# Router logits by 8 products a tile instead of 12, and six tiles' logits planned with a margin

## The chip, the cores and the metric

One core of a Trainium2 chip runs the kernel. The metric is the device time of one execution in microseconds, as the median of several runs; the profile is of one execution of its own.

## The reference

Three layers follow each other. The first is an attention between 512 tokens and 32 state rows, both ways, in 8 batches of 8 heads. Its output, 4352 tokens of 512 values, goes through a dense layer with squared ReLU. The last layer is a mixture of 8 experts in which each token takes one, chosen by logits of normalised vectors:

```
h = x @ w_in; g = relu(h)**2; x = g @ w_out              # 512 -> 2048 -> 512

xn = x / (norm(x) + 1e-6); en = emb / (norm(emb) + 1e-6)
logits = xn @ en.T / tau                                 # 8 experts
e = argmax(logits); w = softmax(logits)[e]
out = w * (relu(x @ w1[e]) @ w2[e])                      # 512 -> 1024 -> 512
```

What the change touches is `xn @ en.T`: for each tile of 128 tokens, 512 values times 8 expert embeddings.

## The kernel before, in words

The 4352 tokens are 34 tiles of 128. Float32 operands are split into a high and a low float16 half, and a product of two such operands is three float16 products (high x high, high x low, low x high) that add up in PSUM.

Up to about 700 us several strands run interleaved. The attention of batch b (`attention`, `state_side`, `state_w`) makes the inputs of two units of 256 tokens: `aT`, transposed by DMA, and `sw` (state times `w_in`, products of line 692). `up1` multiplies them (lines 1387 to 1389, 12 products for two columns of hidden tiles), `hidden` squares the result on ACT and VectorE, and `down1` multiplies by `w_out` (lines 1471 to 1473; the first four tiles in float32, line 1450). Beside this, ACT and VectorE split the experts' weights and write them back to memory (`w_d<-he`). From about 700 us on the second mixture runs: 35 steps of gathered tokens (lines 1781 to 1806).

`route_tile` (line 1204) takes a finished tile of `down1`: ACT squares it and sums (line 1211), VectorE makes a scale, ACT and VectorE split it into two halves (lines 322 and 317), SP issues a DMA transpose into `xr` (line 1225), a single buffer, and TensorE makes the logits: for each of 4 pieces of 128 values, the high half of `xr` times `en_h`, the same times `en_l`, and the low half times `en_h`, all into 8 columns of one PSUM tile (lines 1234 to 1236). VectorE copies them (line 1239). After four tiles `route_group` (line 1243) picks the experts and GpSimd writes the token records.

The order on each engine isn't written out. Each strand is a generator that yields what it needs next: an engine and a duration, an event, or a buffer. `Plan.run` keeps a clock for each engine and takes the strand that can start first by its estimates, then the one with the lower priority number; the instructions are issued to the engines in that order. For TensorE work of strands with a priority from 1.3 to below 5 it adds `MARGIN` (1.75 us) to the time at which the data are believed ready:

```
dep = r[2] if len(r) > 2 else th[2]
if r[0] == "pe" and 1.3 <= th[1] < 5:
    dep += self.MARGIN
key = (max(dep, self.free[r[0]]), th[1])
```

`end` in `down1` starts `route_tile` with priority 2 for tiles 4 to 31, and with 0 for the first four and the last two.

Of the kernel before, what the change touches and what calls it, by code (L numbers as in the profile page):

```python
# [11 lines left out]
F16 = mybir.dt.float16  # L12
# [4 lines left out]
ALU = mybir.AluOpType  # L17
X = mybir.AxisListType.X
# [5 lines left out]
NE, FE = 8, 1024  # L24
# [200 lines left out]
def act(n):  # L225
    return "act", 0.1 + 0.83e-3 * n
# [10 lines left out]
def tiny(k):  # L237
    return "dve", TINY * k


def pe(k, n):
    return "pe", k * max(0.004, n * 0.4163e-3)
# [3 lines left out]
def moe_kernel(  # L246
# [19 lines left out]
    plan = Plan()  # L266
# [4 lines left out]
    const = ctx.enter_context(tc.tile_pool(name="const", bufs=1))  # L271
# [18 lines left out]
    mm = nc.tensor.matmul  # L290
    V = nc.vector
# [3 lines left out]
    def pow2(s, inv, v, K):  # L295

        m = small.tile([128, 4], F32, name="p2m")[:, :v.shape[1]]
        V.tensor_scalar(out=m.bitcast(I32), in0=v.bitcast(I32), scalar1=0x7F000000, scalar2=1,
                        op0=ALU.bitwise_and, op1=ALU.logical_shift_right)
        V.tensor_scalar(out=s.bitcast(I32), in0=m.bitcast(I32), scalar1=-1.0, scalar2=float(K << 23),  # L300
                        op0=ALU.mult, op1=ALU.add)
        V.tensor_scalar(out=inv.bitcast(I32), in0=m.bitcast(I32), scalar1=float((254 - K) << 23), scalar2=None,
                        op0=ALU.add)
# [15 lines left out]
    def split(hi, lo, src, scale, n):  # L319

        yield act(n)
        nc.scalar.activation(out=hi, in_=src, func=AF.Copy, scale=scale)
        yield dve(n)
        split_lo(lo, src, scale, hi)
# [48 lines left out]
    ise = const.tile([128, 2 * NE], F32, name="ise")  # L373
    u1 = const.tile([128, NT], F32, name="u1")
    itau = const.tile([128, 1], F32, name="itau")
    en_h = const.tile([128, 4, NE], F16, name="en_h")
    en_l = const.tile([128, 4, NE], F16, name="en_l")
    cum = const.tile([128, NT + 1, NE], F16, name="cum")
    nc.gpsimd.memset(cum[:, 0, :], 0.0)

# [20 lines left out]
    def ev(*key):  # L401
        return evs.setdefault(key, Ev(plan))
# [801 lines left out]
    def route_tile(i, ps, k_h, rc, st):  # L1204

        j = i % 4
        rc = rc.bitcast(F16)
        if i < 2 * F32U:
            yield ev("wo scale")
        yield act(600)  # L1210
        nc.scalar.activation(out=rc[:, 0:512].bitcast(BF16), in_=ps, func=AF.Square, accum_out=st["f2"][:, j:j + 1],
                             scale=unit if i < 2 * F32U else 1.0)
        yield tiny(4)
        f2 = st["f2"][:, j:j + 1]
        V.tensor_scalar(out=f2, in0=f2, scalar1=FLOOR, scalar2=None, op0=ALU.max)
        s2 = small.tile([128, 1], F32, name="s2")
        pow2(s2, st["is2"][:, j:j + 1], f2, 204)
        if i < 2 * F32U:
            V.tensor_tensor(out=s2, in0=s2, in1=unit, op=ALU.mult)
        yield from split(rc[:, 0:512], rc[:, 512:1024], ps, s2, 600)  # L1220
        d_slots.release(k_h)
        yield xr_slots
        yield "sp", 0.06
        xr = mg.tile([128, 8, 128], F16, name="xr", bufs=XR)
        nc.sync.dma_start_transpose(xr, rc[:, 0:1024])
        plan.cur[2] = plan.dma(1 << 18) + 1.0
        yield ev("en")
        at = plan.now()
        yield t_slots
        plan.cur[2] = max(at, plan.now())  # L1230
        pl = ps_t.tile([128, 512], F32, name="t")
        yield pe(12, NE)
        for k in range(4):
            mm(pl[:, 0:NE], lhsT=xr[:, k, :], rhs=en_h[:, k, :], start=k == 0, stop=False)
            mm(pl[:, 0:NE], lhsT=xr[:, k, :], rhs=en_l[:, k, :], start=False, stop=False)
            mm(pl[:, 0:NE], lhsT=xr[:, 4 + k, :], rhs=en_h[:, k, :], start=False, stop=k == 3)
        xr_slots.release()
        yield tiny(1)
        V.tensor_copy(st["lg"][:, j, :], pl[:, 0:NE])
        t_slots.release()  # L1240
        ev("lg", i).set()

# [162 lines left out]
    def down1():  # L1405
# [25 lines left out]
        def end(i, ps, k_h, rec, st, m):  # L1431
            g = i // 4
            if i % 4 == 0:
                plan.add(group_unscale(g), 1)
            plan.add(route_tile(i, ps, k_h, rec, st), 2 if 2 * F32U <= i < NXT else 0)
            if i % 4 == m - 1:
                plan.add(route_group(4 * g, m, st["recs"], st["k_r"], st), 2 if g < B else 0)
# [491 lines left out]
```

## Time and profile before

| | us |
|---|---|
| median of 3 runs | 1087.84 |
| lowest and highest run | 1084.52, 1088.25 |
| the profiled execution, its own time | 1086.77 |
| span of its trace | 1085.0 |
| TensorE busy in the span | 1042.6 |
| VectorE, ACT, GpSimd busy | 667.6, 593.7, 121.6 |

The busy share of TensorE is of modelled ends, and products overlap: what a product costs is the distance from its start to the next one's. The three lines of the logits have 136 products each, 34 tiles times 4.

### The profile page before, as it was taken

The page shows a single profiled execution, that of the slowest core. Times are in us where ns is not written, and L with a number is a line of the kernel's source. Part 1 is how long each engine was busy: PE and PEld are TensorE (multiplying, and loading weights), DVE is VectorE, ACT ScalarE, POOL GpSimd, SP SyncE. Part 2 cuts the span into 40 slices and gives each one's busy share as a digit, 9 for nine tenths or more (in the row PEclk, how much of TensorE's full clock was granted, in tenths as well). Part 3 has the DMA queues.
Part 4 walks back from the last instruction along what each step waited for, and adds up shares of the span by engine and source line. Part 5 has one row for each costly group of instructions (what it writes and reads, how often), then busy time and mean ns, then how long its engine had stood idle before and what let it go on. Part 6 is the DMA issues. An engine that isn't in the chain of part 4 may idle for free. (4 is left out here: it accounts for less than half of the span.)

```text
span 1085.0 us, 26401 instructions
## 1 busy us (share of the span) xinstructions
PE 1042.6 (96%) x10657; PEld 672.0 (62%) x10657; DVE 667.6 (62%) x1813; ACT 593.7 (55%) x994; POOL 121.6 (11%) x149
## 2 busy tenths in 40 slices
PE   5889999999999999999999999999999999999998
PEld 4445455465565565655655666677777677767674
DVE  6788887767878877887887773575323222222222
ACT  6999985876889887888878683210101010111110
POOL 0000001001002002001010010321112211112111
PEclk9899999999999999999999999999999999999999
DMA  9873275447676877649679288843996666694591
GB/s 301 336 233 81 82 198 167 138 129 181 199 159 192 227 202 210 180 131 253 143 223 290 76 252 281 256 89 104 293 283 166 183 198 215 185 272 156 160 319 66
DMA packets 161313, 211.75 MB, mean 195 GB/s; under 512 B 112226, under 2 KB 115042, under 8 KB 155939
## 3 DMA queue, kind: packets, MB, share of 16 engines
q1 hardware_dynamic: 152434, 182.86, 58.5%
q0 software_dynamic: 8320, 27.08, 7.7%
q8 instruction: 85, 1.39, 0.5%
q14 instruction: 42, 0.34, 0.1%
q10 hardware_dynamic: 432, 0.08, 0.0%
HBM read 257.92 MB, written 51.68 MB: 285 GB/s over the span
## 5 line engine op out<-in xcount | busy, mean ns | idle before, releaser
L1737 ACT ACTIVATE r<-u 128x512 f32<-128x512 f32 x70 | 41.8, 597 | 324.6 <-PE u L1783 300.9
L1473 PE MATMUL d<-wo_t,g 128*128 128x512 f16 x480 | 183.0, 381 | 1.4 <-DVE g L1359 1.4
L1471 PE MATMUL d<-wo_t,g 128*128 128x512 f16 x480 | 183.4, 382 | 0.8 <-DVE g L1357 0.8
L1472 PE MATMUL d<-wo_t,g 128*128 128x512 f16 x480 | 183.1, 381 | 0.0
L1387 PE MATMUL u<-aT,sw 128*128 128x256 f16 x512 | 140.6, 275 | 11.5 <-ACT sw L666 5.9
L1389 PE MATMUL u<-aT,sw 128*128 128x256 f16 x512 | 140.5, 274 | 0.7 <-DVE sw L317 0.7
L1388 PE MATMUL u<-aT,sw 128*128 128x256 f16 x512 | 140.4, 274 | 0.0
L1340 ACT ACTIVATE r<-u,cg 128x512 f32<-128x512 f32 x120 | 81.7, 682 | 67.0 <-PE u L1389 46.2
L1740 DVE CAST hh<-r 128x512 f16<-128x512 f32 x70 | 30.2, 432 | 139.1 <-ACT r L1737 137.1
L1751 DVE TENSOR_SCALAR o<-d,rec,wo_t 128x512 f32<-128x512 f32 x35 | 28.3, 810 | 106.1 <-PE d L1806 100.4
L1359 DVE TENSOR_TENSOR g<-r,g 128x512 f16<-128x512 f32 x120 | 82.4, 688 | 14.4 <-ACT r L1354 12.8
L1313 POOL DMA_INDIRECT rec_d<-rec,pi x34 | 36.4, 1072 | 488.6 <-DVE rec L1309 173.0
L1806 PEld LDWEIGHTS <-hh 128*128 128x128 f16 (+1 forms) x688 | 54.8, 103 | 56.9 <-issue 0.4
L1473 PEld LDWEIGHTS <-g 128*128 128x128 f16 x480 | 47.2, 98 | 59.3 <-DVE g L1359 1.9
L1781 PE MATMUL u<-xes,stage 128*128 128x128 f16 x448 | 75.8, 219 | 0.0
L1783 PE MATMUL u<-xes,stage 128*128 128x128 f16 x448 | 75.8, 219 | 0.0
L1782 PE MATMUL u<-xes,stage 128*128 128x128 f16 x448 | 75.8, 219 | 0.0
L1471 PEld LDWEIGHTS <-g 128*128 128x128 f16 x480 | 47.4, 99 | 45.8 <-DVE g L1357 1.2
L1387 PEld LDWEIGHTS <-sw 128*128 128x128 f16 x512 | 51.2, 100 | 39.4 <-issue 19.3
L1354 ACT ACTIVATE r<-r 128x512 f32<-128x512 f32 x120 | 74.8, 625 | 1.4
L1472 PEld LDWEIGHTS <-g 128*128 128x128 f16 x480 | 47.2, 98 | 44.9 <-issue 1.6
L1781 PE MATMUL u<-xes,xx 128*128 128x128 f16 x416 | 70.5, 219 | 0.0
(333 smaller groups left out, 2648.5 us busy)
## 6 DMA issues: line engine op xcount, KB each, us to landing
w_d<-he SPq DMA_DIRECT2D x128, 256.0 KB
g<-w_d SPq DMA_DIRECT2D x16, 2048.0 KB
wo_t<-w_d SPq DMA_DIRECT2D x16, 2048.0 KB
stage<-w_d SPq DMA_DIRECT2D x14, 2048.0 KB
he<-w_d SPq DMA_DIRECT2D x14, 2048.0 KB
xx<-w_d SPq DMA_DIRECT2D x13, 2048.0 KB
sw<-w_d SPq DMA_DIRECT2D x13, 2048.0 KB
stage<-in_w_dram SPq DMA_DIRECT2D x20, 1024.0 KB
```

The lines of the kernel that those rows point to most:

```text
L1340: nc.scalar.activation(out=r, in_=ps, func=AF.Relu, scale=cg[:, g:g + 1] if u >= F32U else cgq[:, c:c + 1])
L1354: nc.scalar.activation(out=r, in_=r, func=AF.Square)
L1359: V.tensor_tensor(out=gl, in0=r, in1=gh, op=ALU.subtract)
L1387: mm(o, lhsT=hl[:, i, 0, fs], rhs=aT[:, i, :], start=i == 0, stop=False)
L1388: mm(o, lhsT=hl[:, i, 0, fs], rhs=aT[:, 2 + i, :], start=False, stop=False)
L1389: mm(o, lhsT=hl[:, i, 1, fs], rhs=aT[:, i, :], start=False, stop=i == 1)
L1471: mm(ps, lhsT=g_h[:, f, ts], rhs=w[:, 0, :], start=f == 0, stop=False)
L1472: mm(ps, lhsT=g_h[:, f, ts], rhs=w[:, 1, :], start=False, stop=False)
L1473: mm(ps, lhsT=g_l[:, f, ts], rhs=w[:, 0, :], start=False, stop=f == KF - 1)
L1781: mm(p[:, j, xs], lhsT=w[:, 0, k, fs], rhs=xe[:, k, xs], start=k == 0, stop=False)
L1782: mm(p[:, j, xs], lhsT=w[:, 0, k, fs], rhs=xe[:, 4 + k, xs], start=False, stop=False)
L1783: mm(p[:, j, xs], lhsT=w[:, 1, k, fs], rhs=xe[:, k, xs], start=False, stop=k == 3)
```

## The change

The two halves of the embeddings lie side by side in one tile. Per piece of 128 values one product with 16 columns gives high x high and high x low in columns 0 to 15; a second group of four products gives low x high in columns 16 to 23. VectorE adds the three blocks of 8 columns where it copied one. In the same place the strand's priority is raised to at least 1.3 for the logits and what follows in it. The plan's estimate of the products goes from 12 of 8 columns to 8 of 16.

```diff
-    en_h = const.tile([128, 4, NE], F16, name="en_h")
-    en_l = const.tile([128, 4, NE], F16, name="en_l")
+    en = const.tile([128, 4, 2, NE], F16, name="en")
+    en_h, en_l = en[:, :, 0], en[:, :, 1]
...
         pl = ps_t.tile([128, 512], F32, name="t")
-        yield pe(12, NE)
+        plan.cur[1] = max(plan.cur[1], 1.3)
+        yield pe(8, 2 * NE)
         for k in range(4):
-            mm(pl[:, 0:NE], lhsT=xr[:, k, :], rhs=en_h[:, k, :], start=k == 0, stop=False)
-            mm(pl[:, 0:NE], lhsT=xr[:, k, :], rhs=en_l[:, k, :], start=False, stop=False)
-            mm(pl[:, 0:NE], lhsT=xr[:, 4 + k, :], rhs=en_h[:, k, :], start=False, stop=k == 3)
+            mm(pl[:, 0:2 * NE], lhsT=xr[:, k, :], rhs=en[:, k].rearrange("p a e -> p (a e)"), start=k == 0, stop=k == 3)
+        for k in range(4):
+            mm(pl[:, 2 * NE:3 * NE], lhsT=xr[:, 4 + k, :], rhs=en_h[:, k, :], start=k == 0, stop=k == 3)
         xr_slots.release()
         yield tiny(1)
-        V.tensor_copy(st["lg"][:, j, :], pl[:, 0:NE])
+        V.tensor_reduce(out=st["lg"][:, j, :], in_=pl[:, 0:3 * NE].rearrange("p (a e) -> p e a", a=3), axis=X, op=ALU.add)
         t_slots.release()
```

Every later line of the program stands one line lower, so line 1387 is 1388 there. The order of TensorE is the same up to tile 0's logits, differs from there to the second step or so of the second mixture, and is the same again after it.

TensorE around tile 0's logits (`xr`), before: behind the last float32 product of `down1` (L1450), ahead of 24 products that make `S`, which becomes `sw` (L692).

```order
L1450 MATMUL d<-wo_t,g 128x512 x4
L1234 LDWEIGHTS xr
L1234 MATMUL t<-en_h,xr 128x8
L1235 LDWEIGHTS xr
L1235 MATMUL t<-en_l,xr 128x8
L1236 LDWEIGHTS xr
L1236 MATMUL t<-en_h,xr 128x8
...
L692 LDWEIGHTS sthl
L692 MATMUL S_1160<-wi,sthl 32x512
```

And in the changed kernel:

```order
L1451 MATMUL d<-wo_t,g 128x512 x4
L692 LDWEIGHTS sthl
L692 MATMUL S_1159<-wi,sthl 32x512
...
L1235 LDWEIGHTS xr
L1235 MATMUL t<-en,xr 128x16
...
L1237 LDWEIGHTS xr
L1237 MATMUL t<-en,xr 128x8
```

The 24 products of line 692 have moved ahead of the logits.

TensorE ahead of tile 2's logits, before, from the float32 product that ends the tile. Left out between the rows are 36 up products (L1387 to L1389), 12 of line 756, 48 of line 508 and 24 down products (L1471 to L1473), with their loads.

```order
L1450 MATMUL d<-wo_t,g 128x512 x4
L1387 LDWEIGHTS sw
...
L1473 LDWEIGHTS g
L1473 MATMUL d<-wo_t,g 128x512
L1234 LDWEIGHTS xr
L1234 MATMUL t<-en_h,xr 128x8
```

In the changed kernel 30 up products, the same 12 and 48, and 36 down products stand between:

```order
L1451 MATMUL d<-wo_t,g 128x512 x4
L756 LDWEIGHTS sthl
...
L1474 LDWEIGHTS g
L1474 MATMUL d<-wo_t,g 128x512
L1235 LDWEIGHTS xr
L1235 MATMUL t<-en,xr 128x16
```

The logits stand 12 down products later and 6 up products earlier.

SP's queue up to the transposes of tiles 2 and 3 into `xr`, before; `aT` and `he` are transposes of the attention, `stage`, `wo_t` and `xx` loads of 1 MB, `w_d` converted weights going out.

```order
L339 DMA w_d<-he 128x1024 x3
L339 DMA wo_t<-in_w_dram 128x4x512
L339 DMA xx<-in_xS_dram 128x2048
L339 DMA stt<-in_stT_dram 128x256
L1225 DMA_TRANSPOSE xr<-rec_1077 128x8x128
L1225 DMA_TRANSPOSE xr<-rec_1132 128x8x128
L553 DMA_TRANSPOSE aT<-xx 128x8x128
```

And in the changed kernel:

```order
L339 DMA w_d<-he 128x1024
L339 DMA xx<-in_xS_dram 128x2048
L339 DMA stt<-in_stT_dram 128x256
L339 DMA wo_t<-in_w_dram 128x4x512
L339 DMA w_d<-he 128x1024 x2
L1225 DMA_TRANSPOSE xr<-rec_1076 128x8x128
L553 DMA_TRANSPOSE aT<-xx 128x8x128
L779 DMA_TRANSPOSE he<-he 128x16x128
L1225 DMA_TRANSPOSE xr<-rec_1131 128x8x128
```

Two writes of converted weights moved ahead of tile 2's transpose, and two attention transposes ahead of tile 3's.

## Rows read from the trace of the kernel before

**Rows 1.** The page: busy us, share and instructions; then busy tenths in 40 slices.
```profile
PE 1042.6 (96%) x10657; PEld 672.0 (62%) x10657; DVE 667.6 (62%) x1813; ACT 593.7 (55%) x994; POOL 121.6 (11%) x149
...
PE   5889999999999999999999999999999999999998
...
DVE  6788887767878877887887773575323222222222
```
**Rows 2.** Groups by line: names, shapes, count, busy us, mean ns, idle before and releasers.
```profile
L1313 POOL DMA_INDIRECT rec_d<-rec,pi x34 | 36.4, 1072 | 488.6 <-DVE rec L1309 173.0 <-ACT g L1352 128.7 <-DVE p2m L298 70.1
...
L1234 PE MATMUL t<-en_h,xr 128*128 128x8 f16 x136 | 13.5, 167 | 3.4 <-DMA xr<-rec 3.4
...
L1234 PEld LDWEIGHTS <-xr 128*128 128x128 f16 x136 | 11.5, 96 | 8.1 <-DMA xr<-rec 5.3 <-issue 0.9
...
L1239 DVE COPY lg<-t 128x8 f32<-128x8 f32 x34 | 5.5, 162 | 16.6 <-PE t L1236 15.4 <-PE u L1389 1.2
```
**Rows 3.** Timeline at tile 2's logits: start us, us, engine, line, [idle before].
```profile
154.48 0.38 PE L1473 MATMUL d<-wo_t,g 128*128 128x512 f16 x1
...
155.77 0.38 PE L1473 MATMUL d<-wo_t,g 128*128 128x512 f16 x1
...
157.85 0.18 PE L1234 MATMUL t<-en_h,xr 128*128 128x8 f16 x1 [1.70 <-DMA xr<-rec]
157.89 0.17 PE L1235 MATMUL t<-en_l,xr 128*128 128x8 f16 x1
...
158.14 0.17 PE L1236 MATMUL t<-en_h,xr 128*128 128x8 f16 x1
158.17 0.27 PE L1387 MATMUL u<-aT,sw 128*128 128x256 f16 x1
...
158.38 0.27 PE L1389 MATMUL u<-aT,sw 128*128 128x256 f16 x1
```
**Rows 4.** Stretches A:B: length, busy us of each engine, then granted clock (PEclk), DMA.
```profile
109.50:114.50 5.00, 4.91 (x50) 2.65 (x51) 4.86 (x12) 5.00 (x8) 0.00 (x0) 1.00 0.28 52
159.40:162.90 3.50, 3.50 (x11) 1.19 (x9) 3.27 (x7) 3.29 (x6) 0.00 (x0) 0.51 1.03 229
193.50:197.00 3.50, 3.50 (x12) 1.41 (x10) 3.29 (x13) 3.46 (x6) 0.00 (x0) 0.51 0.60 150
```
**Rows 5.** Timeline, TensorE, products of 64 columns one behind the other.
```profile
125.12 0.19 PE L802 MATMUL t<-he,xx 128*128 128x64 f16 x1
...
125.41 0.19 PE L800 MATMUL t<-he,xx 128*128 128x64 f16 x1
```
**Rows 6.** Groups by line, VectorE, the nearest reductions.
```profile
L711 DVE TENSOR_REDUCE gm<-t 128x8 f32<-128x256 f32 x8 | 3.3, 416 | 0.0
...
L1269 DVE TENSOR_REDUCE lm<-l 128x4 f32<-128x32 f32 (+1 forms) x9 | 1.7, 184 | 0.3
```
**Rows 7.** Timeline, TensorE, around tile 0's logits.
```profile
107.39 1.02 PE L1450 MATMUL d<-wo_t,g 128*128 128x512 f32 x2
109.59 0.18 PE L1234 MATMUL t<-en_h,xr 128*128 128x8 f16 x1 [1.18 <-DMA xr<-rec]
...
109.97 0.84 PE L692 MATMUL S<-wi,sthl 64*32 64x512 f16 x24
110.75 0.28 PE L1387 MATMUL u<-aT,sw 128*128 128x256 f16 x1
```
**Rows 8.** Timeline, SP, the transposes of tiles 2 and 3 into `xr`.
```profile
146.68 12.89 SPq L1225 DMA_TRANSPOSE xr<-rec  x2
```
**Rows 9.** Waits of TensorE between 75 and 700 us: total, times, longest.
```profile
PE t L471 <- ACT xx L465: 3.1, 3, 2.1
PE u L1387 <- ACT r L1340: 2.0, 5, 0.7
```
**Rows 10.** Timeline, ACT and TensorE, the attention's sums of squares, third step.
```profile
189.15 0.69 ACT L1340 ACTIVATE r<-u,cg 128x512 f32<-128x512 f32 x1 [2.21 <-PE u L1389]
...
192.41 0.39 PE L471 MATMUL t<-ss,one 128*128 128x3 f32 x2 [2.11 <-ACT xx L465]
```

## The prediction

> **What bounds the kernel now.** Start with the page: TensorE is busy for 1042.6 of 1085.0 us, and nine tenths or more in nearly every slice after the first few [rows 1]. What shortens this kernel is TensorE time: fewer products, a wait of TensorE removed, or a stretch at half clock avoided. Next, what the logits cost there. The groups by line give 136 products at each of three lines with a mean of 167 ns (one of the three stands in [rows 2]), but that is the length of one product in a pipeline. The timeline gives the price: inside tile 2's logits the starts run from 157.89 to 158.14 in ten steps, 25 ns a product, and the next unit's product starts 0.32 us after the first logit product [rows 3]. The same rows show TensorE standing still ahead of them: the last product before starts at 155.77, the first logit product at 157.85, released by the transpose that fills `xr`. Last comes the granted clock. Some 1.5 us after that wait it falls to about half (0.51) for 3.5 us, and does so again after a wait at line 471; after tile 0's shorter wait it stays at 1.00 [rows 4].
>
> **The change, part by part.**
>
> *Fewer products.* Per tile 12 products become 8, four of 16 columns and four of 8. TensorE takes an 8-column product every 25 ns [rows 3] and a 64-column one every 29 ns (ten steps from 125.12 to 125.41) [rows 5]; a 16-column product lies between, and I take 25, the nearer end. Saved: 4 x 25 ns = 0.10 us a tile, over 34 tiles **3.4 us**; at 29 ns for the four wide products it is 0.5 us less. TensorE has work on both sides of nearly every tile's logits, so this comes straight off the end.
>
> The Trainium skill ("TensorE: Matmul & The Clock Gate", section "LDWEIGHTS (loading the stationary operand)") gives a weight load its column count over 1.2 in ns, about 107 ns for these 128 columns. If the loads stood one behind the other, the four dropped ones would save 14.5 us in all by that figure, an estimate from the page. The starts 25 ns apart speak against it: the loads overlap here.
>
> *Copy to reduction.* The copy of 8 logits takes 162 ns [rows 2]. A reduction of 24 values to 8 isn't in the trace; the nearest are 32 values to 4 in 184 ns and 256 to 8 in 416 ns [rows 6]. I take 184: 22 ns x 34 = 0.7 us of VectorE (8.6 us at the far end; it can hardly be cheaper than the copy it replaces). VectorE is busy for seven to eight tenths of each slice in this phase [rows 1], and its free share takes 0.02 us every 17 us. Without that cover the routing of a group and POOL's record writes come later, not TensorE's products. For the sum: nothing. The shared `en` tile adds no instruction.
>
> *Margin for the first four and last two tiles.* Their logits had priority 0, so the planner put them where it believed the data to be ready; from 1.3 on it adds 1.75 us. Two of the six did wait.
>
> Tile 0: of the two float32 products the second starts 0.43 us after the first, at 107.82, so TensorE was free at 108.25; the logits start at 109.59, a wait of 1.34 us [rows 7]. The new order puts the 24 products of line 692 ahead. They held TensorE from 109.97 to 110.75, 0.78 us [rows 7]. If their inputs lie ready, they fill the hole: **0.8 us** saved, 0.6 of the wait stays. Queued behind on TensorE is a unit of up products, which moves up by as much.
>
> Tile 2: the pitch of the products ahead is 0.215 us (six steps from 154.48 to 155.77), so the wait is 157.85 - 155.77 - 0.22 = 1.86 us [rows 3]. The new order has 12 more down products and 6 fewer up products ahead (two steps of those from 158.17 to 158.38, 0.105 each): 12 x 0.215 - 6 x 0.105 = 1.95 us. The wait is covered: **1.9 us**. If TensorE comes earlier (by tile 0's 0.8 and two tiles' 0.2) and the data do not, up to 0.9 us of it stays. With the wait I expect the half clock behind it to go: 3.5 us at 0.51 lose 3.5 x 0.49 = **1.7 us** [rows 4].
>
> On SP, tile 2's transpose took from 146.68 to 157.8 to land, behind loads of 1 MB; in the new order it has the same loads ahead and two more writes of converted weights. Tile 3's transpose, which must wait for tile 2's logits since `xr` is a single buffer (the second of the two in [rows 8]), now stands behind two attention transposes instead of ahead of them: those get away earlier. On POOL, four record writes of about 1.07 us each [rows 2] move in between the first six gathers of the second mixture; the first two gathers stay ahead, and a later one feeds a step that is two or more steps away. Nothing for the sum.
>
> *Everything between.* From tile 0's logits to the start of the second mixture (about 110 to 700 us) the planner picks another order for all attention, up and down products. The products are the same. The waits of TensorE there, outside the logits, are 3.1 us at line 471 and 2.0 at line 1387 [rows 9]; with the half clock behind line 471's (1.7) and single waits of up to 1 us some 8 us can be drawn anew. The bounds: all of it goes (-8), or it doubles (+8). I take 0, as the same kinds of neighbours follow each other in both orders.
>
> **Sum:** 3.4 + 0.8 + 1.9 + 1.7 = 7.8 us. The profiled execution took 1086.8 us and would take 1079.0. The median of the runs, 1087.84, lies 1.1 above it, so my forecast is **1080 us**. A measurement of this kernel can tell about 0.5% (5.4 us) from no change: "faster" begins at 1082.4.
>
> **Rivals.**
>
> *A. The redraw gives back what the margin won.* Waits of the same size appear elsewhere and only the products remain: 1087.8 - 3.4 = 1084.4. For it: the planner that caused the waits of [rows 9] still does not know how long ACT and the transposes take. Against: the two holes removed are covered by named instructions.
>
> *B. Tile 2's transpose lands later still.* It stands behind the same loads; 11.1 us from issue to landing [rows 3, 8] has no fixed relation to a margin of 1.75 us. Wait and half clock stay: 3.4 + 0.8, so 1083.6.
>
> *C. The redraw helps.* Half of the 8 us goes too: 1076.
>
> *D. Slower: the sums of squares of the attention (line 471) get less cover.* Each of seven steps puts this small product on TensorE's queue behind a chain of ACT. At one of them the chain ran from 189.15 to 192.41, 3.3 us, TensorE waited 2.1 us [rows 10] and then had half clock [rows 4]: about 2.1 + 1.7 = 3.8 us a place. In the new order that step has 18 up products, a set of logits and 24 products of line 692 between the unit that feeds the chain and itself, 1.9 + 0.2 + 0.8 = 2.9 us, so some 0.4 us too few; the others have 12 down products (2.6 us) or more. It decides from four new places on: -7.8 + 4 x 3.8 = +7.4, so 1095.2. I see none that is so bare.
>
> *E. Loads in line.* With weight loads as the pitch, at the 96 ns that one takes in the trace [rows 2], the products alone would save 4 x 34 x 96 ns = 13.1 us, with the margin 17.5: 1070.3. The 25 ns pitch is against it.
>
> **How the numbers follow.** Forecast 0.47, A 0.22, B 0.14, C 0.12, D 0.04, E 0.01. Faster by over 0.5%: four fifths of the forecast's chance (it lies only 2.4 us past the bound), C, E and a few hundredths of A and B, which lie 1 to 2 us short of it: 0.56. Slower by over 0.5%: D and the outer end of the redraw, 0.05. The same: 0.39. The range reaches down to C less 2 us for the spread of the runs (1084.5 to 1088.3), 1074, and up to A with that spread and a part of the redraw, 1089. That leaves out D, E and the outer ends of C and A.
>
> **What would show it.** Right: 136 products of 16 columns and 136 of 8, starts 25 ns apart, a tile's logits 0.2 us long; the 24 products of line 692 ahead of tile 0's logits and a wait of some 0.6 us there; no wait over 1 us and no half clock at tile 2; a reduction of about 184 ns. Wrong: the waits at the logits replaced by others between 75 and 700 us, above all at line 471 with half clock behind them, or steps well over 29 ns between 16-column products.

## The result and the profile after

The changed kernel took 1097.29 us (median of 5 runs, 1095.19 to 1100.59) beside 1087.84 us (5 runs, 1084.52 to 1089.74): a ratio of 1.0101, interval 1.0079 to 1.0122. It is 1% slower. The forecast was 1080, in 1074 to 1089.

The page of the changed kernel (busy us, share, count; then busy tenths and granted clock in 40 slices), against [rows 1]:

```profile
PE 1038.3 (95%) x10521; PEld 671.0 (61%) x10521; DVE 668.5 (61%) x1812; ACT 594.5 (54%) x995; POOL 120.8 (11%) x149
...
PE   5889998999999999989989999899999999999998
...
PEclk9899999999999999999999999899999999999999
```

TensorE has 136 products fewer and 4.3 us less busy time, in a span 10.4 us longer (1095.4). The time is in holes. Four slices fell from nine tenths to eight; in one of them, which begins at 685 us, the granted clock fell to eight tenths too.

The logits by line, against [rows 2] (count, busy us, mean ns, idle before):

```profile
L1314 POOL DMA_INDIRECT rec_d<-rec,pi x34 | 36.3, 1067 | 487.4 <-DVE is L302 126.3 <-DVE rec L1310 124.7 <-DVE lg L1240 111.6
L1235 PE MATMUL t<-en,xr 128*128 128x16 f16 x136 | 8.5, 170 | 1.3 <-DMA xr<-rec 1.3
L1237 PE MATMUL t<-en,xr 128*128 128x8 f16 x136 | 8.2, 166 | 0.0
...
L1240 DVE TENSOR_REDUCE lg<-t 128x8 f32<-128x24 f32 x34 | 6.0, 176 | 14.0 <-PE t L1237 13.7 <-PE u L1390 0.2
```

Tile 2's logits, against [rows 3] (timeline, TensorE; merged rows carry their count):

```profile
158.63 0.38 PE L1474 MATMUL d<-wo_t,g 128*128 128x512 f16 x1
158.85 0.25 PE L1235 MATMUL t<-en,xr 128*128 128x16 f16 x4
158.95 0.24 PE L1237 MATMUL t<-en,xr 128*128 128x8 f16 x4
159.05 0.27 PE L1388 MATMUL u<-aT,sw 128*128 128x256 f16 x1
```

Eight products take 0.20 us, 25 ns each, the wide ones too, and nothing waits ahead of them. Tile 0's, against [rows 7]: the 24 products of line 692 stand ahead, a short wait stays.

```profile
108.86 0.84 PE L692 MATMUL S<-wi,sthl 64*32 64x512 f16 x24
110.16 0.26 PE L1235 MATMUL t<-en,xr 128*128 128x16 f16 x4 [0.45 <-DMA xr<-rec]
```

Stretches with the granted clock (the figure after the five engines), against [rows 4]: full around tile 2, half twice near 700 us.

```profile
155.00:165.00 10.00, 10.00 (x97) 6.55 (x96) 8.74 (x20) 9.35 (x17) 0.00 (x0) 1.00 0.70 139
...
697.80:701.20 3.40, 3.40 (x36) 3.40 (x34) 0.75 (x1) 0.00 (x0) 0.00 (x0) 0.51 1.10 329
708.00:711.40 3.40, 3.40 (x36) 3.40 (x34) 0.00 (x0) 0.00 (x0) 0.00 (x0) 0.50 0.74 82
```

TensorE's waits from 75 to 700 us (total, times, longest), against [rows 9]:

```profile
PE u L1388 <- ACT r L1341: 8.4, 8, 3.2
...
PE t L471 <- ACT xx L463: 1.8, 1, 1.8
PE t L1235 <- DMA xr<-rec: 1.3, 2, 0.9
PE t L471 <- ACT xx L465: 1.3, 1, 1.3
```

The waits at the logits fell from 3.4 to 1.3 us, line 471 kept 3.1, and the up products (1387 before, 1388 now) wait 8.4 us for ACT instead of 2.0.

**Where the 10.4 us went.** TensorE's time can be split in two: for each product the median distance to the next start at its line and shape, and the *loss*, what the distances exceed it by (waits, half clock, waits inside a stretch). The medians add up to 995.6 us before and 991.8 after, 3.8 less. The loss, cut at 30 us ahead of the second mixture's first product and 40 us behind it ("the opening"):

| profile | ahead | opening | behind |
|---|---|---|---|
| kernel before | 69.0 | 2.3 | 8.5 |
| changed kernel | 71.2 | 9.9 | 13.0 |

So -3.8 + 2.2 + 7.6 + 4.5 = +10.5. Most lies at the opening, where nothing was forecast. Each row is one execution; how far executions of one order differ is told below the next table. SP's rows at the opening, of the kernel before and of the changed one (start, us on SP):

```profile
658.04 2.18 SPq L339 DMA_DIRECT2D w_d<-he  x2
662.39 0.36 SPq L1687 DMA_DIRECT2D stage<-w_d  x1
664.45 0.34 SPq L1687 DMA_DIRECT2D he<-w_d  x1
...
672.09 0.35 SPq L1687 DMA_DIRECT2D xx<-w_d  x1
686.08 1.25 SPq L1727 DMA_TRANSPOSE xes<-rec  x1
```

```profile
664.76 4.27 SPq L339 DMA_DIRECT2D w_d<-he  x4
671.20 0.37 SPq L1688 DMA_DIRECT2D stage<-w_d  x1
673.25 0.34 SPq L1688 DMA_DIRECT2D he<-w_d  x1
675.11 0.34 SPq L1688 DMA_DIRECT2D xx<-w_d  x1
690.17 1.36 SPq L1728 DMA_TRANSPOSE xes<-rec  x1
...
697.16 0.35 SPq L1688 DMA_DIRECT2D sw<-w_d  x1
697.55 3.08 SPq L1728 DMA_TRANSPOSE xes<-rec  x1
```

The mixture loads its weights (2 MB each) once the last converted expert weight is written (`w_d<-he`): the writes end at 660 us before and 669 now, while TensorE reaches the mixture at about the same time (697.9 and 697.6). GpSimd gathers the first rows at 682.52 before and at 681.05 now:

```profile
682.52 1.06 POOL L1707 DMA_INDIRECT rec<-rec_d,wo_t  x1 [47.89 <-PE u L1396]
```

```profile
681.05 1.07 POOL L1708 DMA_INDIRECT rec<-rec_d,wo_t  x1 [47.10 <-PE t L1293]
```

From that gather to the first transpose of its rows it is 3.6 us before and 9.1 now, with three loads issued 6 to 10 us ahead of it. The transposes land late, and TensorE waits (changed kernel, 650 to 715 us), with half clock behind each wait:

```profile
PE u L1782 <- DMA xes<-rec: 5.0, 2, 2.7
```

### The profile page after: what moved, and what is told of

It is laid out like the page before. It is cut to its first block, busy times and chain, and to the rows that moved or that the text cites. A ratio compares the mean times of both kernels' runs of the same rounds, so it can differ in the third digit from the quotient of the medians.

```text
span 1095.4 us, 26121 instructions
## 1 busy us (share of the span) xinstructions
PE 1038.3 (95%) x10521; PEld 671.0 (61%) x10521; DVE 668.5 (61%) x1812; ACT 594.5 (54%) x995; POOL 120.8 (11%) x149
## 5 line engine op out<-in xcount | busy, mean ns | idle before, releaser
L1473 PE MATMUL d<-wo_t,g 128*128 128x512 f16 x480 | 181.9, 379 | 0.9 <-issue 0.9
L1389 PE MATMUL u<-aT,sw 128*128 128x256 f16 x512 | 140.2, 274 | 0.5 <-issue 0.5
L1782 PE MATMUL u<-xes,stage 128*128 128x128 f16 x448 | 77.4, 221 | 2.3 <-DMA xes<-rec 2.3
L1783 PE MATMUL u<-xes,stage 128*128 128x128 f16 x448 | 77.4, 221 | 0.0
L1784 PE MATMUL u<-xes,stage 128*128 128x128 f16 x448 | 77.4, 221 | 0.0
L1473 PEld LDWEIGHTS <-g 128*128 128x128 f16 x480 | 47.0, 98 | 44.6 <-issue 0.6
```

Source lines behind the costliest of these rows:

```text
L1389: mm(o, lhsT=hl[:, i, 0, fs], rhs=aT[:, 2 + i, :], start=False, stop=False)
L1473: mm(ps, lhsT=g_h[:, f, ts], rhs=w[:, 1, :], start=False, stop=False)
L1782: mm(p[:, j, xs], lhsT=w[:, 0, k, fs], rhs=xe[:, k, xs], start=k == 0, stop=False)
L1783: mm(p[:, j, xs], lhsT=w[:, 0, k, fs], rhs=xe[:, 4 + k, xs], start=False, stop=False)
L1784: mm(p[:, j, xs], lhsT=w[:, 1, k, fs], rhs=xe[:, k, xs], start=False, stop=k == 3)
```

## The experiments

The kernels ran in five groups, each with the kernel before beside it; its median was 1083.4, then 1075.1, 1074.5, 1076.0 and 1075.4 us. So times compare as ratios to the kernel before of the same group. Losses are of one profiled execution each.

### Which part costs: products, margin, or the order

Four kernels with one part each. The diffs are against the kernel before; the eight products with their reduction are those of the change.

```diff
# p8_old_order: eight products, planner as before
         yield pe(12, NE)
# p12_new_order: twelve products, planner as in the change
+        plan.cur[1] = max(plan.cur[1], 1.3)
-        yield pe(12, NE)
+        yield pe(8, 2 * NE)
# p8_no_margin: eight products, the estimate alone
-        yield pe(12, NE)
+        yield pe(8, 2 * NE)
# p12_margin: twelve products, the margin alone
+        plan.cur[1] = max(plan.cur[1], 1.3)
         yield pe(12, NE)
```

> The 8 products, the shared embedding tile and the reduction of the change, but the planner is told what it was told before (12 products of 8 columns, priority 0 for the first four and last two tiles), so that all engines keep the order of the kernel before, instruction by instruction. Theory O (the change lost its time to the new order): 34 x 4 x 25 ns = 3.4 us less than before, 1084.4 us, ratio 0.997; the waits of the kernel before at tile 0 (1.3 us) and tile 2 (1.9 us, with half clock behind it) are there again. Rival P (the new products or the reduction cost more than they save): no faster than before, 1088 us or up to the 1097 of the changed kernel.

Measured: 1.0004 (0.9987 to 1.0022). The gain of the products is not there; a later section looks for it. The wait at tile 0 is there again (1.2 us), the one at tile 2 is not, and the granted clock is 1.00 from 159.4 to 162.9 us, where it was 0.51 [rows 4]. Nor is that wait in before_no_load1 (below), which is the kernel before up to some 670 us. The first logit product of tile 2 in these two (timeline, TensorE), against [rows 3]:

```profile
155.66 0.25 PE L1234 MATMUL t<-en,xr 128*128 128x16 f16 x4
```

```profile
157.20 0.17 PE L1234 MATMUL t<-en_h,xr 128*128 128x8 f16 x1
```

p8_no_margin, before_marg170 and p8_old_pad have the same order of TensorE up to there, and no wait at tile 2 either. Of six profiles with this order only that of the kernel before has it.

> The reverse: 12 products and the copy of the kernel before, but the planner is told what the change tells it, so that all engines have the order of the changed kernel. Theory O: 3.4 us more than the changed kernel, 1100.7 us, ratio to before 1.012; waits for the transposed tokens at the start of the second mixture (2.5 and 2.9 us in the changed kernel), with half clock behind each. Rival P: the time of the kernel before, 1088 us.

Measured: 1.0112 (1.0093 to 1.0132).

> The change without its margin: 8 products, estimated as 8 of 16 columns, priority 0 as before. The order is the kernel before's for the first quarter of TensorE's products, then one of its own. If the margin is what spoils the order (theory M): 1084 us, as the products alone. If every redraw of the order draws the waits anew (theory O): anywhere from 1080 to 1100, and the waits of tiles 0 and 2 as before in any case, since the order there is the same.

Measured: 1.0098 (1.0076 to 1.0119). Theory M falls. Tile 0 waits as before (1.1 us), tile 2 does not.

> The margin alone: 12 products with the estimate of before, priority 1.3. The order is the changed kernel's for the first fifth of TensorE's products, then one of its own. Theory M: as slow as the changed kernel or 3.4 us slower, 1097 to 1101 us. Theory O: anywhere from 1083 to 1103, with tile 2's wait of 1.9 us and its half clock gone in any case and tile 0's about 0.8 us shorter.

Measured: 0.9986 (0.9973 to 0.9999). Theory M falls here too.

| profile | ahead | opening | behind |
|---|---|---|---|
| p8_old_order | 64.7 | 2.7 | 12.5 |
| p12_margin | 60.9 | 3.7 | 9.7 |
| p12_new_order | 70.2 | 8.8 | 9.9 |
| p8_no_margin | 67.4 | 10.9 | 12.6 |

Not every difference between such rows is one of the orders. With the later runs there are several profiles with TensorE in the same order. Ahead, the old order loses 60.7 to 69.0 us in three profiles, the changed one 60.1 to 71.2 in seven (those with idle products at the start left out); behind, 3.4 to 12.5 and 5.7 to 13.0. These ranges overlap. Only the opening is apart: where nothing was edited there, 2.3, 2.7 and 4.3 us in the old order and 9.9, 8.8, 10.3 and 11.9 in the changed one.

The order costs it (theory O; P, that the products do, falls): with the twelve products of before and the new order the kernel is as slow as the changed one. The two orders of twelve products with the margin differ only in the planner's estimate for the logits, 12 x 4 ns = 48 ns in one and 8 x 16 x 0.4163 ns = 53 ns in the other, by the planner's formula. Five nanoseconds a tile, true or not, redraw what follows and are worth 1.3% here. In both slow orders TensorE waits at the opening for the transposed rows; here p12_new_order, p8_no_margin, and p12_margin, where no such wait is left (680 to 715 us):

```profile
PE u L1782 <- DMA xes<-rec: 5.5, 2, 3.9
```

```profile
PE u L1781 <- DMA xes<-rec: 6.7, 2, 5.1
```

```profile
PE u L1782 <- ACT r L1738: 0.8, 1, 0.8
```

In p8_no_margin all six first gathers stand ahead of the record writes on GpSimd, as before, and the rows are late all the same. The four record writes that the change moves in between are not the cause.

### Is any redrawn order that bad, and the fastest kernel

```diff
# before_marg170, after_marg170
-MARG = 1.75
+MARG = 1.7
# p8_est12_margin: the changed kernel, planner told the old cost
-        yield pe(8, 2 * NE)
+        yield pe(12, NE)
```

> The kernel before, with the planner's margin 1.70 us instead of 1.75, and nothing else: an order redrawn by a number that says nothing of the chip. Theory L (a redrawn order lands anywhere by some 1 per cent, by when the last expert weight is written and what queues ahead of the second mixture's first transposes): ratio between 0.995 and 1.012; over 1.006 if TensorE waits more than 3 us for the transposed rows near 690 us, under 1.004 if it does not. Rival (the changed estimate is what costs, not a redraw as such): 0.998 to 1.002.

Measured: 1.0003 (0.9985 to 1.002); opening 3.5 us. Both sides allow it.

> The changed kernel with the planner's margin 1.70 us instead of 1.75: its order redrawn. Theory L: ratio between 0.993 and 1.012, with the same sign to look for: over 1.006 if TensorE waits more than 3 us for the transposed rows near 690 us, under 1.004 if not. Rival (the changed estimate costs 1 per cent by itself in whatever order): 1.008 to 1.012.

Measured: 0.9976 (0.9956 to 0.9996); opening 6.2 us. TensorE waits about 3 us there (2.9 idle, 3.1 from start to start), for `xr` and not for the gathered rows, and the kernel is still faster than before. The sign that theory L gave is too rough.

> Eight products and the margin, but the planner is told the twelve products' cost, so that every engine has the order of the run with the margin alone (0.9986). If the four products fewer a tile are worth what their 25 ns each say (33 tiles, 3.4 us): ratio 0.9955, within 0.994 to 0.997. If other waits take that up, as in the run with eight products in the old order (1.0004): 0.998 to 1.000.

Measured: 0.9957 (0.9938 to 0.9976), the lowest ratio here and faster than both kernels (after_marg170 and p8_est12_pad below are not apart from it beyond their intervals). It has the change's products and margin; only the estimate that the planner works with is the old one. The estimate of the change isn't bad by itself, then: with a margin of 1.70 it goes from 1.0101 to 0.9976. What a redraw gives is not foreseen by the size of the number that caused it.

### Can the opening be mended in the slow order

after_gated and after_gated2 are the changed kernel with the two loads of the mixture's second step issued later on SP, the other engines' rows unmoved; after_again is the changed kernel beside the latter.

```diff
# after_gated: hold the loads of step 1, issue xx behind xes(0) and sw behind xes(1)
+                    if t == 1 and key not in turned:
+                        held[key] = ask
+                    else:
+                        ask()
...
+            if t in held:
+                held.pop(t)()
# after_gated2: both behind xes(0), xr and xes(1)
+            for n in (0, 1) if t else ():
+                if n in held:
+                    held.pop(n)()
```

> The changed kernel with its order of TensorE, VectorE, ScalarE and GpSimd untouched; on SyncE alone two rows move: the weight loads of the mixture's second step (xx<-w_d, sw<-w_d, 2 MB each) stand behind the transposes xes(0) and xes(1) instead of ahead of them. Theory M (the second mixture starts late since its gathered rows and their transposes queue behind 6 MB of weight loads): the waits of 2.46 and 2.86 us at 697.6 and 707.6 and the half clock behind each (3.41 us, so 1.7 us lost each time) go, 8.7 us of some 1097; ratio to the kernel before 1.002, within 1.000 to 1.004. Rival W (the transposes are late for another reason, the four record writes between the gathers above all, or the time comes back later in the mixture): ratio 1.008 to 1.011, the two waits still there or the same time found behind them.

Measured: 1.0072 (1.0047 to 1.0097); opening 11.0 us.

> The changed kernel once more, beside the three others and the kernel before on one chip: ratio 1.010, within 1.008 to 1.012, with the waits of TensorE for the transposed rows near 695 and 705 us (5 us together) and one of some 2.7 us near 1065 us.

Measured: 1.0076 (1.0057 to 1.0095); opening 10.3 us. That is a little below the range given, with an interval that overlaps that of the first measurement (1.0079 to 1.0122). The waits are 2.4 us for `xr` and 2.8 for the gathered rows, and one of 2.8 us near 1052.

> The changed kernel, where SyncE again is the only engine whose rows move: both weight loads of the mixture's second step now stand behind the transposes xes(0), xr and xes(1), as they do in the run with the margin alone, which had no wait over 1 us at this place. In the run with the first shift of these loads the waits moved to the logits (4.9 and 2.3 us for xr, which stood behind the same 2 MB loads). Theory Q (on SyncE's queue, whatever transpose stands behind a 2 MB load is late by it): TensorE's loss between 30 us ahead of the mixture's first product and 40 us behind it falls from 10 to some 4 us; ratio 0.005 to 0.006 below that of the changed kernel in this call, about 1.005. Rival (at this point any place of the loads costs the same, since 8 MB have to come in before the second step): within 0.002 of 1.007.

Measured: 1.0074 (1.0057 to 1.0091); opening 13.9 us.

Theories M and Q fall. The first wait goes to the transposes of the attention's last tiles, the second to those and the weights themselves (680 to 715 us, first after_gated, then after_gated2):

```profile
PE t L1235 <- DMA xr<-rec: 6.9, 2, 4.8
```

```profile
PE u L1794 <- DMA xx<-w_d: 4.6, 1, 4.6
PE t L1235 <- DMA xr<-rec: 3.2, 1, 3.2
```

In both, the wait moved to other transfers on SP, and no time was won.

Next the late writes, and then 2 MB less to load.

```diff
# after_early: the last 14 writes left out, 14 of their size issued among earlier ones
+                if 4 * i + q < 57:
                     yield from load(dst[:, q * 1024:q * 1024 + 1024], hl[:, 0, :], 1 << 18)
...
+                    if 20 <= 4 * i + q < 27:
+                        m = 4 * i + q + 37
...
+                            nc.sync.dma_start(d7[:, c7:c7 + 1024], hl[:, a, :])
# after_no_load1, before_no_load1: xx<-w_d of step 1 replaced
+                    if (t, name) == (1, "w1"):
+                        nc.gpsimd.memset(slots[a], 0.0)
+                    else:
+                        nc.sync.dma_start(slots[a], src[bass.ds(ex * 128, 128)], cond=new)
```

> The changed kernel with the order of all five engines but SyncE untouched; of the 128 writes of converted expert weights the last 14 (3.5 MB, to 661 us) are left out, and 14 others of the same size are issued among the writes at some 420 to 480 us, so that the weights of the last expert are another's (the output is not the reference's). Theory L (the expert weights are written too late in this order, so that the mixture's first weight loads are still in flight when its rows are gathered): the loads of the mixture start 6 us earlier or more, the first gather lands within 6 us instead of 8.7, and TensorE's loss from 30 us ahead of the mixture's first product to 40 us behind it falls from 10 to some 4 or 5 us; ratio 0.005 below that of the changed kernel, 1.002 to 1.004. Rival (the lateness of the writes is a companion, not the cause, and the opening of the mixture in this order has too little other work for TensorE): loss still 8 us or more, ratio 1.007 to 1.010.

Measured: 1.0067 (1.0042 to 1.0092); opening 6.5 us, ahead 64.4. Neither side is shown. The last write now goes out at 643 us, but the loads start only at 663.96, behind two transposes at which SP stands until 661:

```profile
643.87 17.26 SPq L1237 DMA_TRANSPOSE xr<-rec  x2
663.96 0.37 SPq L1700 DMA_DIRECT2D stage<-w_d  x1
```

Set against the first gather, the loads are earlier by 3.7 us (13.5 us ahead of it, 9.8 in after_again). The transposes follow 5.4 us behind it instead of 8.7, and the loss at the opening fell (10.3 to 6.5): in theory L's direction, though not by its 6 us. The time is the same within the intervals. Two stretches at half clock near 417 and 479 us take some of it back; the waits there, at line 471, are in after_again too (2.7 and 2.6 us), without half clock.

> The changed kernel without the weight load xx<-w_d of the mixture's second step (2 MB, the last of the three that are issued 6 to 10 us ahead of the first gather); GpSimd, idle there for 47 us, sets that tile to zero instead, so that the second step, and later ones that keep its weights, multiply by zeros (the output is not the reference's). No other row of any engine moves. Theory T (at the opening the weight loads, the gathered rows and their transposes need more of the DMA engines than the stretch has, and in this order they start too late): TensorE's loss from 30 us ahead of the mixture's first product to 40 us behind it falls from 10 or 12 to 6 us or less, and it stays won: ratio 0.004 to 0.007 below that of the changed kernel, 1.001 to 1.005. Rival (what TensorE lacks there is other work in the order, or the time comes back later): ratio 1.006 to 1.010.

Measured: 1.0096 (1.0073 to 1.012); opening 13.4 us. GpSimd's memset took 6.9 us, and a cast on VectorE beside it, 0.43 us in after_again, did not end before it:

```profile
661.43 6.92 POOL L1689 MEMSET xx<- 128x8192 f16 x1 [35.10 <-DVE he L317]
661.59 7.04 DVE L1358 CAST g<-r 128x512 f16<-128x512 f32 x1 [0.27 <-ACT r L1355]
```

TensorE then waits 3.1 us near 674 for VectorE's squares, with half clock around it.

> The same edit in the kernel before, as the control: its loss at the opening is 2.3 us in the profile shown, so there is nothing to win: ratio 0.998 to 1.002 by every theory; a lower one would say that 2 MB fewer are worth time in any order.

Measured: 1.0054 (1.0035 to 1.0073); opening 9.5 us. As a test of the load both runs say nothing, because of the memset that took its place. In the control it stands among the gathers, and three VectorE instructions beside it take 3 to 4 us each:

```profile
678.49 1.00 POOL L1710 DMA_INDIRECT rec<-rec_d,wo_t  x1 [0.30 <-issue]
679.48 6.95 POOL L1688 MEMSET xx<- 128x8192 f16 x1
686.59 1.01 POOL L1710 DMA_INDIRECT rec<-rec_d,wo_t  x1 [0.17 <-issue]
```

The fourth gather starts 8.1 us behind the third instead of 1.3, TensorE waits 3.9 us for `xr` near 706 us with half clock beside it, and the kernel is 0.54% slower, 5.8 us, where the loss at the opening grew by some 7 (9.5 against 2.3 and 2.7 in the same order). That was not meant, but it shows what the opening is worth: here the time lost there was not won back later.

### Where eight products in the old order lost their gain

p8_old_order should have shown 3.4 us and showed none. The kernel before was not profiled beside it. Its profile has a wait that the kernel before's first profile has not, ended by nothing that the trace shows (timeline, TensorE), with half clock behind it:

```profile
1049.75 0.19 PE L1782 MATMUL u<-xes,g 128*128 128x64 f16 x1
1052.86 0.20 PE L1783 MATMUL u<-xes,g 128*128 128x64 f16 x1 [2.91 <-issue]
```

p8_est12_margin (3.1 us, with half clock) and the changed kernel (2.7, without in its first profile; 2.8 with in after_again) have it too; p12_margin and p12_new_order have 0.8 at most; before_marg170 and before_no_load1, with twelve products too, have 1.8 and 2.1 without half clock. With 272 instructions fewer on TensorE by then, each later one has another place in the program.

```diff
# p8_old_pad, p8_est12_pad, after_pad
                     yield pe(6, 256)
+                    if (u, c, ff) == (0, 0, 0):
+                        for _ in range(136):
+                            mm(ps[:, 1, 0:8], lhsT=oneb, rhs=oneb[:, 0:8], start=True, stop=True)
```

> Eight products in the order of the kernel before (1.0004), with 136 idle products of 8 columns put ahead of the first U1 product near 22 us, where TensorE waits 5 us anyway: TensorE's program has as many instructions as with twelve products, so that from 700 us on each instruction has the place in the program that it had before. Theory F (the wait of 3.1 us near 1050 us, ended by nothing that the profile shows and 2.5 us behind the start of a 16 KB packet of the instruction queue, is TensorE out of instructions, and where it falls is set by the place of the instructions in the program): the wait and its half clock (1.7 us) go, ratio 0.9965, within 0.995 to 0.998. Rival (the wait belongs to the work of that step): still 3 us near 1050, ratio 1.000.

Measured: 0.9985 (0.9969 to 1.0001); no such wait.

> The same 136 idle products in the kernel with eight products, the margin and the planner's old cost (0.9957, a wait of 3.1 us and a half clock near 1045 us). Theory F: both go, ratio 0.991 to 0.993. Rival: 0.9957 as without them.

Measured: 0.996 (0.9945 to 0.9975); the wait is 1.55 us, without half clock.

> The changed kernel with the 136 idle products near 22 us. Theory F (a late packet of instructions): the wait of 2.8 us near 1052 to 1068 us and its half clock shrink to 1.5 us or less, as they did in the two other kernels with these products, which is worth 1.3 to 4.5 us; less what the idle products may cost at the start, ratio 1.004 to 1.008. Rival: the wait stays, ratio 1.0076 to 1.010.

Measured: 1.0048 (1.0028 to 1.0068); the wait is still 2.4 us, with half clock. The time lies in theory F's range, but not by its mechanism.

Theory F isn't shown: the wait goes in one kernel, halves in another and stays in the third, which behind the last tile's logits (some 715 us) has instruction for instruction the places of p12_new_order, where it was 0.8. What sets it stays open. The times are 0.002 and 0.003 lower than without the idle products in the first and the third, no lower in the second, each within the intervals or nearly; they do not follow the wait.

## Why the prediction was wrong

**Fewer products: right in the trace, hardly to be seen in the time.** 136 of 16 columns and 136 of 8, starts 25 ns apart, 0.20 us a tile. The medians fall by 3.3 us in the old order (995.6 to 992.3) and by 3.8 in that of p12_margin (995.3 to 991.5), against 3.4 forecast. Of that the time shows -0.0029 (0.9986 to 0.9957) in one pair of equal order and +0.0004 in the other. The wait at 1053 us with its half clock would be large enough to take it there, but p8_est12_margin has the same wait (p12_margin has not) and shows the gain all the same: what took it is open. The Trainium skill's weight load of its column count over 1.2 in ns ("TensorE: Matmul & The Clock Gate", section "LDWEIGHTS (loading the stationary operand)", some 107 ns) is no pitch here either: each of the 25 ns steps has its own load.

**Reduction: right.** 176 ns for the 184 taken, and VectorE's busy time rose by 0.9 us where 0.7 was worked out. TensorE never waited for it.

**Tile 0: right.** The 24 products of line 692 fill the hole and its wait fell from 1.34 us to 110.16 - 108.86 - 0.78 = 0.5.

**Tile 2: right in the changed kernel, but priced from one execution.** Tile 2 waits for nothing there, with no half clock behind it. But of six profiles with the old order at this place only the one that the prediction read has the wait, and with it the half clock. The 1.9 + 1.7 us stood in that execution and not, as far as profiles show, in the kernel. Without them the prediction's own sum is 4.2 us, which makes 1083.6. Of the writes of converted weights no more stand ahead of tile 2's transpose in the new order than in the old: six in both, two of which moved behind loads of 1 MB.

**The step that failed: "Everything between ... I take 0".** The new order was given gains at tiles 0 and 2, 4.4 us, and no cost elsewhere. With the twelve products of before it costs 12 us, those gains included (p12_new_order, 1.0112 of 1083.4). That is more than the bound of 8 that stood there, and 0 was chosen with no better reason than that the neighbours are of the same kind.

What is clear of the spread between executions is the opening. The step ended at 700 us with no term for it. Of SP the prediction counted the transposes of tiles 2 and 3 and the writes near them; it did not ask when the last of the 128 writes ends, though the mixture's weight loads stand behind it. POOL's record writes, the one thing costed there, did no harm. The opening cost 7.6 us in the first two profiles (2.3 to 9.9) and alone would have turned the forecast's gain into nothing.

Up to the opening the loss rose by 2.2 us where 4.4 of gain were forecast. The spread of one order is larger than that, so what the redraw took there is open. The largest piece in the changed kernel's first profile is line 1388, whose waits for ACT went from 2.0 to 8.4 us; they are 7.5 in p12_new_order, but 2.0 to 3.2 in the six other profiles of this order. Rival A named such waits, with a size that was too small. Rival D looked for them at line 471, which kept its 3.1 us there and has 2.1 to 6.4 in the others.

What is shown: the order causes the loss (p12_new_order), and in one case time lost at the opening stayed lost (before_no_load1). What is seen in the traces and not shown by an experiment: that the loss at the opening comes from the late end of the writes. In the orders that ran as planned, where the first weight load is issued 15 to 24 us ahead of the first gather, the transposes follow the gather by 3.5 to 3.6 us and the opening loses 2.3 to 5.1; where it is 8 to 10 us ahead, they follow by 8.7 to 9.6 and it loses 8.8 to 11.9; after_marg170 lies between (11.6, 7.4 and 6.2), and after_early fits. Against it as the whole cause: in after_gated and after_gated2 the transposes follow by 3.9 and 4.4 us, and the opening loses 11.0 and 13.9. Why this order is the bad one among its neighbours, row by row, and the 4.5 us behind the opening stay open; in after_again the loss behind it is 5.8 us instead of 13.0.

## What to carry to other kernels

Where a planner orders the work by estimates, a change of an estimate is a change of the whole schedule: measure the edit first with the planner's old numbers, and the new order first with the old edit. A kernel tuned on one order has the luck of that order in it; a few neighbouring values of a planner's number (here a margin of 1.70 or an estimate of 48 ns) tell what is the edit and what is the draw, and the best of them can simply be kept. When costing such a change, follow each queue to the next place where everything must be there at once, and ask what comes last. And before a wait is priced from a profile, look for it in a second execution: here 3.6 of the 7.8 us forecast hung on a wait that five other profiles of the same order do not have.

## What was not expected of the hardware

The half clock does not follow the length of a wait alone. In the kernel before it came behind 1.86 us at tile 2; in the changed kernel the longest wait before the opening, 3.25 us at 559.6 us, has none behind it:

```profile
559.64 0.27 PE L1388 MATMUL u<-aT,sw 128*128 128x256 f16 x1 [3.25 <-ACT r L1341]
```

In p12_new_order the same wait (3.1 us at 560.5) has it, 3.4 us at 0.51 from 561.9.

A memset on GpSimd held VectorE: beside one of 6.92 us a cast of 0.43 us took 7.04 (after_no_load1).

And TensorE can stand for 1.6 to 4 us in the middle of a step of 64-column products with nothing that the profile shows to release it, at nearly the same step in 14 of the 18 profiles. Half clock stood beside nine of these waits (2.4 us and 2.8 to 4.0) and not beside the other five (1.6 to 2.1 us, and 2.7 in the changed kernel).
